# Batch 1's second products as two sweeps over units, weight sums moved forward, and copies of w_in placed behind moves of x

## The chip, the cores and the metric

The kernel runs on one core of one Trainium2 chip. The metric is the device time of one launch in microseconds (us). The engines are TensorE (PE in the profile, with its weight loads as PEld), VectorE (DVE), ScalarE (ACT), GpSimd (POOL) and SyncE (SP), which here only issues DMA transfers. Three timed runs of the kernel before took 632.97 to 633.55 us, median 633.14.

## The reference

An attention between a sequence and a small state, in both directions, and a feed-forward layer on all rows of both results:

```python
B, H, S, Ns, D = (8, 8, 512, 32, 64)
a = softmax(scale * x @ state^T);   xread = a @ state      # rows 0..511 of a batch
a2 = softmax(scale * state @ x^T);  sread = a2 @ x         # rows 512..543
rows = concatenate([xread, sread], axis=2).transpose(0, 2, 1, 3).reshape(B * 544, 512)
h = rows @ w_in                     # 512 -> 2048
g = h * tanh(log(1 + exp(h)))       # mish
out = g @ w_out                     # 2048 -> 512
```

All is fp32 with inputs in memory as 64-bit floats for the weights, which the kernel turns into fp32 by itself.

## The kernel before, in words

Every operand of the two large products is split into a high part, rounded to TensorE's fp32r form, and the low rest; a product is three matmuls (high by high, high by low weights, low by high weights).

xread is never made: state @ w_in is formed per batch (swp in PSUM, from the tiles bd and w_in; parts swh, swl or sw), and the **first product** multiplies it by the softmax weights (tiles ah, al) into the banks ph. There are 8 slots per batch (SLOTS), each of two banks of 128 hidden features for 512 rows: 12 matmuls of 512 columns.

The **second product** goes from mish's output to the banks acc. Batch 0 and batch 1 do it slot by slot for all four blocks of 128 rows (gemm2, line 670): tiles g, gh, gl, half a slot at a time (half_slot, line 1067, and the list `pending`). Later batches do it in two sweeps of 256 rows (p = 0, 1) over **units** (key, p, j): 256 features by 256 rows of slot j. A unit is made by mish (mish_k), prepared (prepare, line 966: high and low parts, tiles gh and gl of tag "g", six buffers) and multiplied (consume, line 1013). A unit in **eight blocks** takes 4 block pairs of 3 matmuls of 512 columns. A unit in **seven products** uses Strassen-like sums: POOL adds blocks of the unit (sums), and 7 products of 3 matmuls of 256 columns replace the 8; in sweeps where all slots are sevens, two matmuls of the seventh product are joined into one of 512 columns (merged). `sevens(key, p)` says how many slots of a sweep are sevens: none in batch 1, 5 in both sweeps of batch 2, 6 and 7 in batch 3's, all 8 later.

Sevens need sums of the weights: seven_weights(j), steps T0 to T7 (line 909). One addition on DVE, four of 256 columns on POOL (j below 4) or DVE, two casts on ACT into the rest of wo and into a tile wx, and the low parts on DVE. The wx of the first slots lies in the buffer of w_in_sb (tag "w_in"), the later ones in those of tags "x" and "sw2". Batches from 2 on read w_in from a copy in DRAM, w_in_again, which four DMAs of 1 MB write (steps w0 and w1 of batch 1, line 1169).

The order of each of PE, DVE, ACT and POOL is the program's order: the class InOrder chains every instruction to the one before it on its engine. Batch 0 follows a list of steps; batches 1 and later follow TABLE (line 1075), one row of steps per slot: G0 and G1 are the halves of the first product, M0 and M1 mish, S and N state @ w_in, X and XD the transposes of x and their moves by eight DMAs (x_turned to x_rows, line 307), SC the scores from x_rows, mm, ee, tr, ex, no, pr the two softmaxes, tu the transposes u and 16 DMAs to e2T, sr the product sread, P and p the preparation of a unit, A and B one half slot or unit each, h and l the high and low part of a slot of batch 1, T the weight sums, w the copies and loads of w_in, lx and li loads of x. Upper case steps belong to the batch that follows. DMA issues on SP have no such chain: a planner orders them from its own estimates, within data dependences and the marks set with `behind(...)`.

Of the kernel before, what the change touches and what calls it, by code (L numbers as in the profile page):

```python
# [9 lines left out]
F32 = mybir.dt.float32  # L10
# [7 lines left out]
P = 128  # L18
# [8 lines left out]
LAG = 2  # L27
WARM = 5
UNITS = 10
SEVEN = 8  # L30
FIRST = 5
G = 4 * P


# [47 lines left out]
def state_attention_mish_kernel(ctx, tc, x, state, w_in, w_out, out):  # L82
# [193 lines left out]
    def attention(b, sn, x_in=None):  # L276
# [689 lines left out]
    def prepare():  # L966
# [46 lines left out]
    def consume():  # L1013
# [8 lines left out]
        if j == max(n7, SLOTS - 2):  # L1022
# [7 lines left out]
        for j, i, hi, lo, a, bank, to, w in steps:  # L1030
# [36 lines left out]
    def half_slot(key, j, at):  # L1067
# [4 lines left out]
        elif ready and (ready[0][:2] != (key, 0) or ready[0][2] < j + (j == SLOTS - 1 and at)):  # L1072
# [1 line left out]

    TABLE = {
        1: """
            G0 M0 G1 M1 z0 z1 mm0 mm1 ee0 ee1 A z0 z1 h l X0 X1 ee0 ee1
            G0 M0 G1 M1 S2 S2 h S2 X2 X3 XD tu w0 B l ST w1
            G0 M0 G1 M1 h A B l
            G0 M0 G1 M1 h A S4 S6 S4 S4 S6 S6 B l T0  # L1080
            G0 M0 G1 M1 h SC sr0 sr1 T0 SC A sr0 sr1 SC MM0 MM1 lx w2 B l T0 TR0 TR1 TR0 TR1 T1
            G0 M0 G1 M1 EE0 EE1 EX0 EX1 T1 h A w3 B l T1 NO EE0 EE1 T2 NO
            G0 M0 G1 M1 h A PR0 PR1 B l
            G0 M0 G1 M1 h PR0 PR1 A N0 PR0 PR1 N0 N0 T2 B l li""",
        2: """
            G0 M0 G1 M1 X0 X1 X2 X3 T2 A T3
            G0 M0 G1 M1 S2 S2 S2 T3 XD B ST T3 A T4
            G0 M0 G1 M1 T4 w4 P p B P p T4 T4
            P G0 M0 p G1 M1 P p A S4 SC S4 S4 SC w5 P p tu B MM0 MM1
            P G0 M0 p G1 M1 P p TR0 TR1 A P TR0 TR1 p B  # L1090
            P G0 M0 p G1 M1 S6 P p S6 S6 EE0 EE1 EX0 EX1 A sr0 sr1 w2 w3 EE0 EE1 P p sr0 sr1 B NO""",
        3: """
            P G0 M0 p G1 M1 P p X0 X1 A P X2 X3 p B
            P G0 M0 p G1 M1 S2 P p S2 S2 XD A ST P p B
            P G0 M0 p G1 M1 P p w4 A P p B
            P G0 M0 p G1 M1 P p A S4 SC S4 S4 SC lx w5 P p B MM0 MM1
            P G0 M0 p G1 M1 P p TR0 TR1 A P TR0 TR1 p T5 B T5
            P G0 M0 p G1 M1 S6 sr0 sr1 P p S6 S6 sr0 sr1 EE0 EE1 EX0 EX1 A w2 w3 EE0 EE1 P p T5 B NO T5
            P G0 M0 p G1 M1 P p NO TU PR0 PR1 A P p B""",
        4: """  # L1100
            P G0 M0 p G1 M1 P p X0 X1 A T6 P X2 X3 p B T6
            P G0 M0 p G1 M1 S2 P p S2 S2 XD A ST T6 P p B
            P G0 M0 p G1 M1 P p T6 w4 A P p B
            P G0 M0 p G1 M1 P p A S4 SC S4 S4 SC lx w5 P p B MM0 MM1
            P G0 M0 p G1 M1 P p TR0 TR1 A P TR0 TR1 p T7 B T7
            P G0 M0 p G1 M1 S6 sr0 sr1 P p S6 S6 sr0 sr1 EE0 EE1 EX0 EX1 A w2 w3 EE0 EE1 P p B T7 NO
            P G0 M0 p G1 M1 P p T7 NO TU PR0 PR1 A P p B""",
        "steady": """
            P G0 M0 p G1 M1 P p X0 X1 A P X2 X3 p B
            P G0 M0 p G1 M1 S2 P p S2 S2 XD A ST P p B  # L1110
# [32 lines left out]
    for key in [*range(1, B - 1), "s", B - 1]:  # L1143
# [22 lines left out]
        def again(n):  # L1166
            if key == 1 and n < 2:
                for g in range(2 * n, 2 * n + 2):
                    nc.sync.dma_start(w_in_again[:, :, g * G:(g + 1) * G], w_in_sb[:, :, g * G:(g + 1) * G])
            else:  # L1170
                of, g = ((key + 1, n - 2), (key, n - 2))[n > 3]
                wis[of, g] = load_w_in_again(g)
# [18 lines left out]
            phs[k] = gemm1(key, j, aTs[key], sw, (k,))[0]  # L1191

        def mish_k(j, k):
            if key == 1:
                if k == 0:
                    gs[j] = new_g(f"1_{j}")
                take_g(gs[j], k, phs[k])
                return
# [5 lines left out]
        def high_1(j):  # L1204
            g = gs.pop(j)
            gs[j] = (g, *high_g(f"1_{j}", g, act.copy))

        def low_1(j):
            g, gh, gl = gs.pop(j)
            low_g(g, gh, gl)  # L1210
            pending.append((1, (2 * j, 2 * j + 1), (gh, gl), NT))
# [56 lines left out]
```

## Time and profile before

| | |
|---|---|
| timed runs, median | 633.14 us (632.97 to 633.55) |
| profiled execution | 633.97 us, span of its instructions 632.1 us |
| PE busy | 623.7 us, 99% |
| PEld busy | 530.3 us, 84% |
| DVE busy | 444.9 us, 70% |
| ACT busy | 357.9 us, 57% |
| POOL busy | 200.5 us, 32% |
| q1, the DMA queue of SP and ACT's issues | 87.58 MB, 44.1% of 16 engines |

Busy time counts a matmul until its modelled end, though the next one has started; so the start times in a timeline tell more of TensorE's pace than busy time does. "idle before <-" names what ended an engine's wait. SPq and ACTq rows are DMA issues: their duration is that of the issue, and the transfer lands later. All instructions stand under line 74, the helper that issues them, so rows are told apart by tiles.

### The profile page before, as it was taken

The page shows a single profiled execution, that of the slowest core. Times are in us where ns is not written, and L with a number is a line of the kernel's source. Part 1 is how long each engine was busy: PE and PEld are TensorE (multiplying, and loading weights), DVE is VectorE, ACT ScalarE, POOL GpSimd, SP SyncE. Part 2 cuts the span into 40 slices and gives each one's busy share as a digit, 9 for nine tenths or more (in the row PEclk, how much of TensorE's full clock was granted, in tenths as well). Part 3 has the DMA queues.
Part 4 walks back from the last instruction along what each step waited for, and adds up shares of the span by engine and source line. Part 5 has one row for each costly group of instructions (what it writes and reads, how often), then busy time and mean ns, then how long its engine had stood idle before and what let it go on. Part 6 is the DMA issues. An engine that isn't in the chain of part 4 may idle for free.

```text
span 632.1 us, 13547 instructions
## 1 busy us (share of the span) xinstructions
PE 623.7 (99%) x5323; PEld 530.3 (84%) x5323; DVE 444.9 (70%) x762; ACT 357.9 (57%) x722; POOL 200.5 (32%) x309
## 2 busy tenths in 40 slices
PE   8999999999999999999999999999999999999997
PEld 6777677787788788888988888888889889898897
DVE  5999786366776873977877873869487777635264
ACT  4999676345465543555447554655456666544442
POOL 0000000123333051323532463336522743443284
PEclk9999999999999999999999999999999999999999
DMA  8999913540465153534554165524555333321000
GB/s 317 412 321 349 324 64 103 139 135 18 106 200 183 34 160 105 171 127 122 142 166 136 33 174 144 181 67 125 143 175 164 106 91 110 101 67 29 7 34 34
DMA packets 71711, 88.77 MB, mean 140 GB/s; under 512 B 13792, under 2 KB 48608, under 8 KB 71648
## 3 DMA queue, kind: packets, MB, share of 16 engines
q1 hardware_dynamic: 71024, 87.58, 44.1%
q8 instruction: 42, 0.69, 0.4%
q10 hardware_dynamic: 624, 0.33, 0.2%
q14 instruction: 21, 0.17, 0.1%
HBM read 62.85 MB, written 13.11 MB: 120 GB/s over the span
## 4 chain that ended last, share of the span: by engine, by line
PE 86%; DMA 5%; DVE 4%; ACT 1%; SPq 1%; issue 1%; POOL 0%; DVEq 0%
PE ph L74 26%; PE acc_top L74 12%; PE acc_one L74 10%; PE acc L74 10%; PE acc_two L74 10%; PE acc_end L74 6%; PE swp L74 5%; PE ph_s L74 3%; DMA w_in_again<-w_in_sb 2%; DMA wir<-in_moe_w_in_dram 2%; DMA wor<-in_moe_w_out_dram 1%; PE srp L74 1%; PE acc_s_one L74 1%; PE acc_s_top L74 1%; PE acc_s_two L74 1%; PE sc L74 1%
## 5 line engine op out<-in xcount | busy, mean ns | idle before, releaser
L74 POOL TENSOR_TENSOR sums<-u 128x256 f32<-128x256 f32 x87 | 70.4, 809 | 230.4 <-DVE gl L74 152.3
L74 ACT ACTIVATE u<-ph 128x256 f32<-128x256 f32 x192 | 63.2, 382 | 85.1 <-PE ph L74 82.9
L74 POOL TENSOR_TENSOR sums<-sums,u 128x128 f32<-128x128 f32 x174 | 100.5, 578 | 13.6
L74 DVE TENSOR_TENSOR gl<-u,gh 128x384 fp32r<-128x384 f32 (+1 forms) x96 | 58.9, 613 | 45.0 <-ACT gh L74 44.1
L74 DVE TENSOR_TENSOR gl<-sums,gh 128x512 fp32r<-128x512 f32 x87 | 66.6, 766 | 29.3 <-ACT gh L74 29.3
L74 PE MATMUL acc<-wo,gh 128*128 128x512 f32 x256 | 80.3, 395 | 0.0
L74 PE MATMUL acc_top<-wo,gh 128*128 128x256 f32 (+1 forms) x384 | 77.8, 294 | 0.0
L74 ACT CAST gh<-u 128x384 fp32r<-128x384 f32 x87 | 44.7, 514 | 55.3 <-PE acc_end L74 38.8
L74 PE MATMUL ph<-ah,swh 128*128 128x512 f32 (+1 forms) x228 | 70.7, 392 | 0.0
L74 PE MATMUL ph<-al,swh 128*128 128x512 f32 (+1 forms) x228 | 70.3, 389 | 0.2 <-DVE al L74 0.2
L74 PE MATMUL ph<-ah,swl 128*128 128x512 f32 (+1 forms) x228 | 70.0, 388 | 0.0
L74 ACT CAST gh<-sums 128x512 fp32r<-128x512 f32 x87 | 54.1, 622 | 26.2 <-POOL sums L74 25.9
L74 PEld LDWEIGHTS acc_top<-wo,gh 128*128 128x128 f32 x384 | 60.5, 191 | 2.7 <-DVE gh L74 0.8
L74 POOL TENSOR_TENSOR w_sums<-w_sums 128x256 f32<-128x256 f32 x16 | 13.0, 811 | 156.3 <-DMA sn<-in_state_dram 123.3
L74 PEld LDWEIGHTS acc<-wo,gh 128*128 128x128 f32 x256 | 47.3, 188 | 13.3 <-issue 3.3
L74 DVE TENSOR_TENSOR swl<-swp,swh 128x512 fp32r<-128x512 f32 (+1 forms) x60 | 36.4, 646 | 29.2 <-ACT swh L74 29.1
L74 PE MATMUL acc_top<-wo,gl 128*128 128x256 f32 (+1 forms) x192 | 56.3, 293 | 0.0
L74 PEld LDWEIGHTS ph<-al,swh 128*128 128x128 f32 x228 | 42.5, 188 | 10.6 <-DVE al L74 1.2
L74 PEld LDWEIGHTS ph<-ah,swl 128*128 128x128 f32 x228 | 42.6, 188 | 9.4 <-DVE swl L74 0.3
L74 PE MATMUL acc<-wo,gl 128*128 128x512 f32 x128 | 49.9, 390 | 0.0
L74 PEld LDWEIGHTS ph<-ah,swh 128*128 128x128 f32 x228 | 39.7, 188 | 8.5 <-issue 0.8
L74 ACT CAST swh<-swp 128x512 fp32r<-128x512 f32 (+1 forms) x60 | 30.5, 562 | 22.7 <-PE swp L74 22.7
(232 smaller groups left out, 1397.5 us busy)
## 6 DMA issues: line engine op xcount, KB each, us to landing
w_in<-w_in_again SPq DMA_DIRECT2D x27, 1024.0 KB, 6.2
x<-in_x_dram SPq DMA_DIRECT2D x32, 256.0 KB, 4.3
wir<-in_moe_w_in_dram SPq DMA_DIRECT2D x16, 512.0 KB, 10.1
wor<-in_moe_w_out_dram SPq DMA_DIRECT2D x16, 512.0 KB, 9.8
x_rows<-x_turned SPq DMA_DIRECT2D x56, 128.0 KB, 2.4
x_in<-in_x_dram SPq DMA_DIRECT2D x24, 256.0 KB, 3.1
out_dram<-sums SPq DMA_DIRECT2D x23, 256.0 KB, 5.3
w_in_again<-w_in_sb SPq DMA_DIRECT2D x4, 1024.0 KB, 9.5
```

Source lines behind the costliest of these rows:

```text
L74: made = method(*args, **kwargs)
```

## The change

- Batch 1 joins the unit scheme: `todo` starts at batch 1, h, l and the tile g go, its mish writes units.
- `sevens`: batch 1 has 0 and 4 (FIRST), batch 2 has 7 and 8, all later sweeps 8.
- All eight-block units get their high part from ACT (before: DVE).
- A sweep without sevens uses two banks only, and its results are copied out of them.
- Weight sums: all subtractions on POOL; T0 to T7 stand between batch 1's slot 3 and batch 3's slot 1 (before: T5 in batch 3, T6 and T7 in batch 4). Tags "x" and "sw2" change places.
- Batch 1's u is made in slot 0 (before: slot 1), and all 16 DMAs to e2T are SP's (before: 4 on ACT). Batch 2's u is made in batch 1's slot 6 (before: batch 2's slot 3).
- The copies w0 and w1 stand behind the last move of x traced before them: w0 behind batch 1's, w1 behind batch 2's.

```diff
-SEVEN = 8
-FIRST = 5
+FIRST = 4
...
-            u = pool.tile([P, 4, 2, NT * NS], F32, tag={0: "u0", 1: "wt", 2: "sw2"}.get(b, "sc"), name=f"u_{b}", bufs=1)
+            u = pool.tile([P, 4, 2, NT * NS], F32, tag={0: "u0", 1: "wt"}.get(b, "sc"), name=f"u_{b}", bufs=1)
...
-                    (nc.scalar if b == 1 and 4 * q + c < 4 else nc.sync).dma_start(
+                    nc.sync.dma_start(
...
-        tag, first, count = ("w_in", 0, 16) if q < 16 else ("x", 16, 4) if q < 20 else ("sw2", 20, 4)
+        tag, first, count = ("w_in", 0, 16) if q < 16 else ("sw2", 16, 4) if q < 20 else ("x", 20, 4)
...
-        by = pool_e if j < 4 else dve
-        if j > 3:
-            yield
-        by.tensor_sub(w[:, 0], w[:, 0], w[:, 1])
...
+        yield
+        pool_e.tensor_sub(w[:, 0], w[:, 0], w[:, 1])
...
-    for key in [*range(2, B - 1), "s", B - 1]:
+    for key in [*range(1, B - 1), "s", B - 1]:
...
     def sevens(key, p):
-        return {2: FIRST, 3: FIRST + 1 + p}.get(key, SEVEN)
+        return {(1, 0): 0, (1, 1): FIRST, (2, 0): SLOTS - 1}.get((key, p), SLOTS)
...
         else:
-            dve.tensor_copy(hi[:, :4], u)
+            act.copy(hi[:, :4], u)
             low_g(u, hi[:, :4], lo[:, :4])
...
-            spans[key, p] = {n: second_bank(f"acc_{key}_{p}_{n}") for n in ("one", "two", "top", "end")}
+            names = ("one", "two", "top", "end")
+            spans[key, p] = {n: second_bank(f"acc_{key}_{p}_{n}") for n in names[0 if sevens(key, p) else 2:]}
...
+        if not sevens(key, t // 2):
+            if "out" not in spans[key, t // 2]:
+                spans[key, t // 2]["out"] = pool.tile([P, 2, DM], F32, tag="g", name=f"o_{key}_{t}", bufs=6)
+            o = spans[key, t // 2]["out"][:, t % 2]
+            (dve.tensor_copy if t % 2 else act.copy)(o, acc)
+            store(key, t, o)
+            return
...
         1: """
-            G0 M0 G1 M1 z0 z1 mm0 mm1 ee0 ee1 A z0 z1 h l X0 X1 ee0 ee1
-            G0 M0 G1 M1 S2 S2 h S2 X2 X3 XD tu w0 B l ST w1
-            G0 M0 G1 M1 h A B l
-            G0 M0 G1 M1 h A S4 S6 S4 S4 S6 S6 B l T0
-            G0 M0 G1 M1 h SC sr0 sr1 T0 SC A sr0 sr1 SC MM0 MM1 lx w2 B l T0 TR0 TR1 TR0 TR1 T1
-            G0 M0 G1 M1 EE0 EE1 EX0 EX1 T1 h A w3 B l T1 NO EE0 EE1 T2 NO
-            G0 M0 G1 M1 h A PR0 PR1 B l
-            G0 M0 G1 M1 h PR0 PR1 A N0 PR0 PR1 N0 N0 T2 B l li""",
+            G0 M0 G1 M1 z0 z1 mm0 mm1 ee0 ee1 A z0 z1 ee0 ee1 tu X0 X1
+            P G0 M0 p G1 M1 w0 S2 S2 S2 X2 X3 XD B ST w1
+            P G0 M0 p G1 M1
+            P G0 M0 p G1 M1 S4 S6 A S4 S4 S6 S6 T0 T0
+            P G0 M0 p G1 M1 SC sr0 sr1 SC A sr0 sr1 SC MM0 MM1 w2 lx TR0 TR1 TR0 TR1
+            P G0 M0 p G1 M1 T0 EE0 EE1 EX0 EX1 A T0 P p w3 B NO EE0 EE1 NO T1 T1
+            P G0 M0 p G1 M1 A P p TU PR0 PR1 T1 T1 B
+            P G0 M0 p G1 M1 N0 PR0 PR1 T2 T2 P p N0 N0 PR0 PR1 A T2 li P p T2 B""",
         2: """
-            G0 M0 G1 M1 X0 X1 X2 X3 T2 A T3
-            G0 M0 G1 M1 S2 S2 S2 T3 XD B ST T3 A T4
-            G0 M0 G1 M1 T4 w4 P p B P p T4 T4
...
+            P G0 M0 p G1 M1 T3 P p T3 X0 X1 A P X2 X3 p B T3
+            P G0 M0 p G1 M1 S2 T3 P p S2 S2 XD A ST P p B
+            P G0 M0 p G1 M1 P p w4 A T4 P p T4 B
+            P G0 M0 p G1 M1 T4 P p A S4 SC S4 S4 SC w5 P p T4 B T5 MM0 MM1
...
+            P G0 M0 p G1 M1 P p X0 X1 A P X2 X3 p T7 B
+            P T7 G0 M0 p G1 M1 S2 P p S2 S2 XD A T7 ST P p T7 B
...
                 for g in range(2 * n, 2 * n + 2):
-                    nc.sync.dma_start(w_in_again[:, :, g * G:(g + 1) * G], w_in_sb[:, :, g * G:(g + 1) * G])
+                    with behind("move"):
+                        nc.sync.dma_start(w_in_again[:, :, g * G:(g + 1) * G], w_in_sb[:, :, g * G:(g + 1) * G])
```

## Rows read from the trace of the kernel before

**Rows 1.** Two stretches of the table of busy times (stretch and length in us, then busy us and instructions of PE, PEld, DVE, ACT and POOL, the granted clock as a share, the DMA engines' share and GB/s), and the longest wait of PE between 15 and 500 us (us in total, times, longest).
```profile
100.00:180.00 80.00, 80.00 (x573) 63.03 (x558) 51.08 (x82) 38.58 (x70) 19.42 (x24) 1.00 0.39 111
180.00:340.00 160.00, 160.00 (x1491) 137.70 (x1490) 121.04 (x217) 83.17 (x192) 49.58 (x80) 1.00 0.46 135
...
PE sc L74 <- DMA x_rows<-x_turned: 1.2, 2, 0.7
```

**Rows 2.** The same table for three shorter stretches.
```profile
36.00:62.00 26.00, 26.00 (x140) 20.12 (x139) 24.40 (x33) 25.78 (x29) 0.00 (x0) 1.00 1.00 352
62.00:66.00 4.00, 2.82 (x38) 1.29 (x36) 2.98 (x3) 3.40 (x6) 0.00 (x0) 1.00 0.63 139
...
104.00:120.00 16.00, 16.00 (x127) 12.62 (x126) 5.43 (x9) 6.41 (x11) 0.00 (x0) 1.00 0.47 132
```

**Rows 3.** Timeline of PE (start us, length us, engine, line, operation, tiles, count): the first row of two half slots of batch 1 and the row behind them, and the same for a unit in seven products of a later batch.
```profile
106.38 0.62 PE L74 MATMUL acc<-wo,gh 128*128 128x512 f32 x2
...
111.82 0.62 PE L74 MATMUL ph<-ah,sw 128*128 128x512 f32 x2
...
303.40 0.40 PE L74 MATMUL acc_one<-wo,gh 128*128 128x256 f32 x2
...
305.92 0.63 PE L74 MATMUL ph<-ah,swh 128*128 128x512 f32 x2
```

**Rows 4.** Timeline of SP's DMA issues: two copies of w_in, and batch 1's moves of x.
```profile
36.28 0.64 SPq L1169 DMA_DIRECT2D w_in_again<-w_in_sb  x1
...
48.93 0.56 SPq L1169 DMA_DIRECT2D w_in_again<-w_in_sb  x1
...
54.09 9.05 SPq L307 DMA_DIRECT2D x_rows<-x_turned  x8
```

**Rows 5.** The chain of waits between 55 and 100 us (start, length, what).
```profile
48.93 12.31 DMA w_in_again<-w_in_sb
...
66.88 7.42 DMA wor<-in_moe_w_out_dram
...
80.39 1.42 PE swp L74 x32
```

**Rows 6.** SP's issues of batch 2's moves and of 12 of batch 1's transfers to e2T, and the time from issue to landing of the moves between 50 and 190 us.
```profile
104.15 5.51 SPq L307 DMA_DIRECT2D x_rows<-x_turned  x8
109.77 7.53 SPq L404 DMA_DIRECT2D e2T<-u  x12
...
DMA to landing us min/median/max: 2.3/2.5/8.0
```

**Rows 7.** Timeline of PE around batch 1's scores.
```profile
62.83 0.39 PE L74 MATMUL acc<-wo,gl 128*128 128x512 f32 x1
63.91 0.59 PE L74 MATMUL sc<-x_rows,bd 64*32 64x256 f32 x2 [0.69 <-DMA x_rows<-x_turned]
64.99 1.09 PE L74 MATMUL sc<-x_rows,bd 64*32 64x256 f32 x30 [0.49 <-DMA x_rows<-x_turned]
```

**Rows 8.** Timeline of DVE in batch 1's first two slots: batch 0's srds, the first of four small steps, and batch 1's u.
```profile
96.43 0.47 DVE L74 TENSOR_SCALAR srds<-srp,rs 128x64 f32<-128x64 f32 x2
...
101.11 0.11 DVE L74 TENSOR_SCALAR sm<-sm 128x1 f32<-128x1 f32 x1
...
104.04 1.26 DVE L74 STREAM_TRANSPOSE u<-e 128x512 f32<-128x512 f32 x2
```

**Rows 9.** Timeline of PE: slot 2's first product, the two swp of slot 3, and batch 2's first product.
```profile
103.66 0.62 PE L74 MATMUL ph<-ah,sw 128*128 128x512 f32 x2
...
117.36 1.96 PE L74 MATMUL swp<-w_in_sb,bd 64*32 64x256 f32 x64
...
158.30 0.77 PE L74 MATMUL ph<-ah,swh 128*128 128x512 f32 x2
```

**Rows 10.** Timeline of ACT: a table load, the last two of the four exps behind it, ah, the longer cast of a weight sum, and the mish of a half slot of batch 2.
```profile
136.12 1.28 ACT L74 ACT_TABLE_LOAD   x1
...
138.84 1.14 ACT L74 ACTIVATE e<-e 128x512 f32<-128x512 f32 x2
...
156.41 1.14 ACT L74 CAST ah<-at 128x512 fp32r<-128x512 f32 x2
...
158.72 0.84 ACT L74 CAST wx_w_in<-w_sums 128x768 fp32r<-128x768 f32 x1
...
160.15 0.66 ACT L74 ACTIVATE u<-ph 128x256 f32<-128x256 f32 x2 [0.59 <-PE ph L74]
```

**Rows 11.** Timeline of POOL: two of its groups for the weight sums.
```profile
124.61 3.17 POOL L74 TENSOR_TENSOR w_sums<-w_sums 128x256 f32<-128x256 f32 x4 [123.31 <-DMA sn<-in_state_dram]
...
151.60 4.37 POOL L74 TENSOR_TENSOR w_sums<-w_sums 128x256 f32<-128x256 f32 x4 [8.33 <-DVE w_sums L74]
```

**Rows 12.** Timeline of DVE: the reduce that begins the first softmax's sums, the two multiplications by the reciprocals, the addition of a weight sum, and al.
```profile
147.46 0.68 DVE L74 TENSOR_REDUCE s<-e 128x16 f32<-128x512 f32 x1
...
149.13 0.69 DVE L74 TENSOR_TENSOR e<-e,r 128x512 f32<-128x512 f32 x1
...
150.25 1.20 DVE L74 TENSOR_TENSOR w_sums<-wo 128x1024 f32<-128x1024 f32 x1
...
151.65 1.23 DVE L74 TENSOR_TENSOR e<-e,r 128x512 f32<-128x512 f32 x1
...
157.06 1.29 DVE L74 TENSOR_TENSOR al<-at,ah 128x512 fp32r<-128x512 f32 x2 [1.69 <-ACT ah L74]
```

More of the change, by code (lines that the diff above doesn't have):

```diff
@@ L913, in seven_weights @@
             w.rearrange("p (k e) c -> p k (e c)", k=2), as_f32(wo[j][:, :, 0]), as_f32(wo[j][:, :, 1]))
-        by = pool_e if j < 4 else dve
-        if j > 3:
-            yield
-        by.tensor_sub(w[:, 0], w[:, 0], w[:, 1])
-        by.tensor_sub(w[:, 1], w[:, 3], w[:, 1])
-        by.tensor_add(w[:, 3], w[:, 3], w[:, 0])
-        by.tensor_sub(w[:, 2], w[:, 2], w[:, 3])
+        yield
+        pool_e.tensor_sub(w[:, 0], w[:, 0], w[:, 1])
+        pool_e.tensor_sub(w[:, 1], w[:, 3], w[:, 1])
+        pool_e.tensor_add(w[:, 3], w[:, 3], w[:, 0])
+        pool_e.tensor_sub(w[:, 2], w[:, 2], w[:, 3])
         yield
@@ L1000, in sums_of @@
     def sums_of(key, p, banks):
-        tag, bufs = ("g", 6) if (key, p) in ((B - 3, 1), (B - 2, 0)) else ("wt", 1)
+        tag, bufs = ("g", 6) if (key, p) in ((1, 1), (B - 3, 1), (B - 2, 0)) else ("wt", 1)
         e = banks["sums"] = pool.tile([P, 4, 256], F32, tag=tag, name=f"sums_{key}_{p}", bufs=bufs)
@@ L1018, in consume @@
         if j == 0:
-            spans[key, p] = {n: second_bank(f"acc_{key}_{p}_{n}") for n in ("one", "two", "top", "end")}
+            names = ("one", "two", "top", "end")
+            spans[key, p] = {n: second_bank(f"acc_{key}_{p}_{n}") for n in names[0 if sevens(key, p) else 2:]}
         banks = spans[key, p]
         n7 = sevens(key, p)
-        if j == max(n7, SLOTS - 2):
+        if n7 and j == max(n7, SLOTS - 2):
             sums_of(key, p, banks)
@@ L1044, in consume @@
             if j == SLOTS - 1 and i == (5 if n7 > j else 1):
-                late.append((key, 2 * p, banks["top"], banks["sums"][:, ::2], ALU.add))
+                late.append((key, 2 * p, banks["top"], n7 and banks["sums"][:, ::2], ALU.add))
             if j == SLOTS - 1 and i == (6 if n7 > j else 3):
-                late.append((key, 2 * p + 1, banks["end"], banks["sums"][:, 1::2], ALU.subtract))
+                late.append((key, 2 * p + 1, banks["end"], n7 and banks["sums"][:, 1::2], ALU.subtract))
             if (key, p) != (B - 2, 0):
@@ L1085, in state_attention_mish_kernel @@
-        2: """
-            G0 M0 G1 M1 X0 X1 X2 X3 T2 A T3
-            G0 M0 G1 M1 S2 S2 S2 T3 XD B ST T3 A T4
-            G0 M0 G1 M1 T4 w4 P p B P p T4 T4
-            P G0 M0 p G1 M1 P p A S4 SC S4 S4 SC w5 P p tu B MM0 MM1
-            P G0 M0 p G1 M1 P p TR0 TR1 A P TR0 TR1 p B
-            P G0 M0 p G1 M1 S6 P p S6 S6 EE0 EE1 EX0 EX1 A sr0 sr1 w2 w3 EE0 EE1 P p sr0 sr1 B NO""",
-        3: """
[L1093 to L1107, printed above, removed]
+            G0 M0 G1 M1 z0 z1 mm0 mm1 ee0 ee1 A z0 z1 ee0 ee1 tu X0 X1
@@ new lines, in state_attention_mish_kernel @@
+            P G0 M0 p G1 M1 w0 S2 S2 S2 X2 X3 XD B ST w1
[5 more added lines that the diff above has]
+            P G0 M0 p G1 M1 N0 PR0 PR1 T2 T2 P p N0 N0 PR0 PR1 A T2 li P p T2 B""",
+        2: """
+            P G0 M0 p G1 M1 T3 P p T3 X0 X1 A P X2 X3 p B T3
+            P G0 M0 p G1 M1 S2 T3 P p S2 S2 XD A ST P p B
+            P G0 M0 p G1 M1 P p w4 A T4 P p T4 B
+            P G0 M0 p G1 M1 T4 P p A S4 SC S4 S4 SC w5 P p T4 B T5 MM0 MM1
+            P T5 G0 M0 p G1 M1 P p TR0 TR1 A T5 P TR0 TR1 p T5 B
+            P G0 M0 p G1 M1 S6 sr0 sr1 P p S6 S6 sr0 sr1 EE0 EE1 EX0 EX1 A T6 w2 w3 EE0 EE1 P T6 p B NO
+            P G0 M0 p G1 M1 P p T6 NO T6 TU PR0 PR1 A P p B
+            P G0 M0 p G1 M1 N0 PR0 PR1 P p N0 N0 PR0 PR1 A li P p B""",
@@ L1108, in state_attention_mish_kernel @@
+        3: """
+            P G0 M0 p G1 M1 P p X0 X1 A P X2 X3 p T7 B
+            P T7 G0 M0 p G1 M1 S2 P p S2 S2 XD A T7 ST P p T7 B
+            P G0 M0 p G1 M1 P p w4 A P p B""",
         "steady": """
@@ L1193, in mish_k @@
         def mish_k(j, k):
[L1194 to L1198, printed above, removed]
             for p in range(2):
@@ L1202, in mish_k @@
                     u[:, 1 - k].rearrange("f h t -> f (h t)"), phs[k][:, p * 2 * P:(p + 1) * 2 * P], AF.Mish)
[L1204 to L1211, printed above, removed]
         def visit_sw(i):
@@ L1220, in state_attention_mish_kernel @@
             run = {
-                "G": lambda k: first_k(j, k), "M": lambda k: mish_k(j, k), "h": lambda _: high_1(j), "l": lambda _: low_1(j),
+                "G": lambda k: first_k(j, k), "M": lambda k: mish_k(j, k),
                 "P": lambda _: begin(), "p": lambda _: end(),
```

## The prediction

> **What bounds the kernel now.** I read the page's busy shares first, then the table of stretches, then TensorE's own waits, then the chain of waits where TensorE did wait, and only then the timelines of single engines. The reader is to see that TensorE is the bound nearly everywhere: 80.00 of 80 us between 100 and 180, 160.00 of 160 in the stretch behind it, always at a granted clock of 1.00, the upper of its two levels (2.4 GHz) [rows 1]. Between 15 and 500 us its only wait worth naming is 1.2 us for the turned rows of x [rows 1]. Since a busy matmul row overlaps the next one, I price TensorE by the distance between starts and not by busy time.
>
> Two things can therefore change the time: matmuls that disappear, and waits of TensorE that appear or go. The stretch from 36 to 66 us is the one with a visible wait, and there the DMA engines are full: share 1.00 at 352 GB/s from 36 to 62 us [rows 2].
>
> **Part 1, seven products instead of eight.** A unit in eight blocks costs 12 matmuls of 512 columns. Two of them run from 106.38 to 111.82, so 2.72 us each. A unit in seven products costs 21 matmuls of 256 columns, 303.40 to 305.92, 2.52 us [rows 3]; the form that joins two of its matmuls has the same columns, and I take the same price. So each unit that changes form gives 0.20 us. Units in eight blocks before: 16 of batch 1 (eight slots, each worth two units), 3 and 3 of batch 2, 2 and 1 of batch 3, together 25. After: 8 in batch 1's first sweep, 4 in its second, 1 in batch 2's first, together 13. Twelve units at 0.20 us are **2.4 us** off TensorE. All of them lie where TensorE has no gap, so all 2.4 us count unless something new is late.
>
> **Part 2, the copies of w_in.** Three of the four 1 MB copies are issued between 36.28 and 48.93 us, ahead of the eight moves of x that begin at 54.09 [rows 4]. At the 352 GB/s of that stretch each holds the DMA engines for 1.05/0.352 = 3.0 us. The third lands 12.31 us after its issue, at 61.24, and the chain of waits goes from it straight into SP's moves [rows 5]. The moves take 9.05 us to issue, where batch 2's eight take 5.51 in a quiet stretch [rows 4, 6]. Without the copies ahead of them the moves still can't start before 54.09, when DVE has just made the last x_turned, but then end near 59.6 and land 2.5 later [rows 6], about 62.1. TensorE wants them at 63.16: the matmul that starts at 62.83 holds it for 0.23, and the change of form takes 0.1. Before, the scores start at 63.91, break off after two instructions (0.07) and resume at 64.99: 0.75 + 1.01 = **1.8 us** of stall that can go [rows 7].
>
> What is late next? The same chain goes on from SP through the last load of w_out (wor, 7.42 us to land), ACT and DVE, to TensorE's swp at 80.39 [rows 5]. TensorE can keep its 1.8 us at 80 only if that load lands as much earlier. It stands behind the moves (same buffer), which end 3.5 us earlier on SP (63.14 against 59.6). If SP puts the two released copies right behind the moves, they take some 5.8 us of DMA time, of which the stretch from 62 to 66 us (share 0.63, 139 GB/s [rows 2]) can take a part; my estimate is that wor lands 1 to 4 us earlier. I take the full 1.8; bounds 0 and 2.2, the upper one with 0.4 lost around 80.39, where swp takes 1.42 us instead of about 1.1.
>
> The other two copies now follow batch 2's moves near 115 us, where the DMA share is 0.47 [rows 2]. Nothing on TensorE stands behind them but T0's write, which is a rival below.
>
> **Part 3, batch 1's new order.** Four units (10.9 us of TensorE) go out of batch 1 into batch 2, so ACT, DVE and SP have that much less cover in batch 1. Two deadlines decide, both on the clock of before.
>
> *Batch 2's moves.* The transposes u now stand in slot 0, before x's: DVE ends srds at 96.9, then some 0.5 of small steps and 1.26 for u, so u is ready at 98.7 instead of 105.3; x's transposes end near 104.1 as before [rows 8]. SP then issues 16 of e2T at 7.53/12 = 0.63 us (four of them stood on ACT's queue) to 108.9, and the moves behind them, 5.5 us, the last landing near 116.4 [rows 6]. On TensorE slot 2 starts at 103.66, a first product takes 2.72 (to 106.38); then another one, swp at 1.96, a unit at 2.8 and a third first product: scores at 116.7 [rows 3, 9]. Slack 0.3 us. If SP mixes in two stores, 0.5 us each, the stall is 0.7; if the moves overtake e2T, none. I take 0.2.
>
> *The end of batch 1.* The longest chain I find, in program order: slot 5's last mish can start at 124.6; T0's casts 1.1, table load and exps 3.9, a cast 0.6 [rows 10]; DVE: a low part 0.7, the sums' reduces and reciprocals 3.7, T1's addition 1.2 [rows 12]; POOL 3.17 [rows 11]; ACT: T1's casts 1.1, four mish 1.3, ah 1.1, a cast 0.5, swh 1.0 [rows 10]; DVE: the rest of swl 1.4 and al 1.2 [rows 12]: 146.5. Batch 2's first product starts at 147.4 (158.30 less 10.9 [rows 9]), and needs al 0.45 later. Slack 1.3 us, so no stall; bounds 0 and 3 us, if POOL's groups and DVE's long instructions stretch. ACT also takes over a 0.6 us cast per eight-block unit from DVE and loses four DMA issues; both lie under TensorE here.
>
> *POOL.* The subtractions of T4 to T7 go from DVE to POOL at 3.17 us a slot [rows 11], and four more units want its sums; batch 2 is over 65 us long, and POOL was busy 49.58 of 160 us [rows 1]. Cost 0, DVE being relieved by about as much; with the cover gone, 1 us a slot. In the rows POOL's group at 151.60 took 4.37 us, not 3.17, while DVE's multiplication of two SBUF tiles took 1.23 instead of 0.69 [rows 11, 12]. The Trainium skill (SBUF — State Buffer, Who interferes with whom) has a rule for it: a DVE instruction with two SBUF inputs and a GpSimd instruction that reads SBUF exclude each other; the trace agrees. By that rule the work given to POOL costs DVE too, and the time would be rival 2's.
>
> **The sum.** 2.4 + 1.8 - 0.2 = 4.0 us. The profiled execution took 633.97 us, its span 632.1; it becomes 629.97. The median of the timed runs is 633.14, 0.83 below that execution, so I forecast **629.1 us**.
>
> **The rivals.**
> 1. *The copies give nothing*: wor lands no earlier, and TensorE gives the 1.8 us back at 80.39, or SP's order keeps other loads ahead of the moves. For it: the chain through wor [rows 5]. Against it: three copies less in the queue. Then 2.4 stays: 630.7.
> 2. *Batch 1 gets too short for ACT, DVE and POOL*: POOL's groups at 4.37 instead of 3.17, twice on the chain to al and to the first sevens, and three DVE instructions that stretch by 0.5, 3.9 us in all, less 1.3 of slack: 2.5 us of stall, 631.6. For it: the stretched rows [rows 11, 12]. Against it: POOL is busy 19.42 of 80 us in that stretch, ACT 38.58 [rows 1].
> 3. *Slower: T0 waits for the late copies.* T0's casts write the buffer of w_in_sb, which the two copies behind batch 2's moves still read. ACT reaches T0 at 125.2; every us that they land later goes down the chain above, past its 1.3 us of slack. Issued at 115 they land by 122 at 3.0 us each. Behind a full queue, at the 12.31 us of the third copy [rows 5], and after SP's loads of sn, w_in and x (issued from 118 on before), it is 134: 134 - 125.2 - 1.3 = 7.5 us, 633.14 - 4.0 + 7.5 = 636.6. It decides from a landing at about 132 on. Against it: the share of 0.47 [rows 2].
>
> **How the numbers follow.** Chances: forecast 0.46, rival 1 0.22, rival 2 0.20, rival 3 0.12. A measurement here tells changes over 0.2%, 1.3 us, so faster is under 631.87. The forecast and nearly all of rival 1 are faster, rival 2 (631.6, give or take 1.5) about half: 0.46 + 0.21 + 0.10 = 0.77. The same: 0.01 + 0.09 + 0.03 = 0.13. Slower: 0.01 + 0.09 = 0.10. The range runs from 1 us under the forecast (the 0.4 at 80 us, 0.6 for a stall that I don't see) to 632.6, which holds most of rival 2.
>
> **What would show it.** Right: no wait for x_rows near 63 us; swp near 80 at 1.1 us; batch 2's scores without a stall; batch 2's first product about 12.7 us earlier than at 158.30 (10.9 moved, 1.8 gained); 2.4 us less TensorE time in second products. Wrong: TensorE waiting for al, gl or x_rows between 100 and 165 us; ACT waiting for a w_in_again copy; wor landing at 74 again.

## The result and the profile after

The changed kernel takes 637.39 us (six executions, 635.20 to 638.72) where the kernel before takes 632.99 beside it: ratio 1.0063, 95% interval 1.0044 to 1.0082. It is slower by some 4 us, and the forecast was 4 us faster. A second comparison on another chip (the run a_again below) gave 1.0076, 1.0060 to 1.0092. The profiled execution took 638.72 us, span 636.9.

All helper rows now stand under line 73, SP's moves under 306, the copies of w_in under 1165. First the page's shares, which answer to the table of before:

```profile
PE 624.0 (98%) x5407; PEld 533.7 (84%) x5407; DVE 449.1 (71%) x764; ACT 369.1 (58%) x767; POOL 240.1 (38%) x361
```

Then TensorE's waits between 100 and 230 us (what waited for what: total us, times, longest), and the table of stretches that answers to [rows 1], with the stretch behind the longest wait apart:

```profile
PE acc_one L73 <- DVE wx_w_in L73: 2.1, 1, 2.1
PE acc_top L73 <- ACT gh L73: 1.1, 1, 1.1
PE srp L73 <- ACT u L73: 0.8, 1, 0.8
PE acc_end L73 <- DVE o L73: 0.5, 1, 0.5
PE sc L73 <- issue: 0.3, 1, 0.3
PE acc_one L73 <- DVE gl L73: 0.2, 1, 0.2
```

```profile
100.00:180.00 80.00, 76.79 (x559) 61.83 (x558) 51.41 (x83) 39.72 (x89) 29.84 (x38) 0.98 0.50 148
180.00:340.00 160.00, 158.06 (x1464) 137.09 (x1462) 121.74 (x206) 88.80 (x201) 77.53 (x114) 1.00 0.41 124
...
166.00:171.00 5.00, 5.00 (x23) 4.41 (x22) 3.22 (x5) 1.04 (x3) 0.32 (x1) 0.66 0.46 97
```

Before, TensorE was busy for all of the first two stretches; now 3.2 and 1.9 us are missing, behind DVE and ACT, and in five microseconds the mean granted clock is 0.66. PE's timeline at the places of [rows 7], [rows 5] and [rows 9]:

```profile
63.47 1.09 PE L73 MATMUL sc<-x_rows,bd 64*32 64x256 f32 x32
...
79.02 1.11 PE L73 MATMUL swp<-w_in_sb,bd 64*32 64x256 f32 x32
...
115.09 0.62 PE L73 MATMUL sc<-x_rows,bd 64*32 64x256 f32 x2
116.02 1.09 PE L73 MATMUL sc<-x_rows,bd 64*32 64x256 f32 x30 [0.31 <-issue]
...
146.65 0.62 PE L73 MATMUL ph<-ah,swh 128*128 128x512 f32 x2
```

Batch 1's scores are one row of 32 without a break, swp near 80 takes 1.11 us instead of 1.42, and batch 2's first product starts 11.65 us earlier (12.7 forecast). SP's issues that answer to [rows 4, 6] show the moves of both batches, with the copies behind them:

```profile
54.33 6.04 SPq L306 DMA_DIRECT2D x_rows<-x_turned  x8
...
61.57 0.61 SPq L1165 DMA_DIRECT2D w_in_again<-w_in_sb  x1
...
96.98 11.06 SPq L403 DMA_DIRECT2D e2T<-u  x16
108.14 5.21 SPq L306 DMA_DIRECT2D x_rows<-x_turned  x8
...
114.72 1.29 SPq L1165 DMA_DIRECT2D w_in_again<-w_in_sb  x2
```

Batch 1's moves are issued by 60.4 instead of 63.1. Batch 2's stand behind sixteen e2T transfers and end at 113.35, where TensorE reaches the scores at 115.09; their landing costs it 0.9 us. Up to here the forecast holds but for that. The loss lies in batch 2. Batch 3's first product, before and now:

```profile
219.11 0.62 PE L74 MATMUL ph<-ah,swh 128*128 128x512 f32 x2
...
224.84 0.62 PE L73 MATMUL ph<-ah,swh 128*128 128x512 f32 x2
```

From batch 2's first product to this took 60.8 us before (from 158.30) and takes 78.2 now (from 146.65), where 60.8 plus the 10.9 moved in, less 1.2 saved there (six units that change form), would be 70.5. The largest piece is seen in TensorE's timeline around unit (1,1,3):

```profile
162.88 0.38 PE L73 MATMUL acc_one<-wx_w_in,gh 128*128 128x256 f32 x1
165.32 0.38 PE L73 MATMUL acc_one<-wx_w_in,gh 128*128 128x256 f32 x1 [2.06 <-DVE wx_w_in L73]
...
168.03 1.05 PE L73 MATMUL ph<-ah,swh 128*128 128x512 f32 x2
168.89 1.05 PE L73 MATMUL ph<-al,swh 128*128 128x512 f32 x2
...
170.84 0.62 PE L73 MATMUL ph<-al,swh 128*128 128x512 f32 x2
```

One matmul that reads the high part of slot 3's weight sum runs, and the next, which reads the low part, comes 2.44 us later instead of 0.12. Behind it, pairs of 512 columns take 1.05 us instead of 0.62: from about 166.7 to 170.1 us the granted clock was at its lower level (1.2 GHz), which costs half of that, 1.7 us. What the low part waited for stands on POOL, ACT and DVE (with T2's group and al, the rows that answer to [rows 11, 12]):

```profile
142.61 3.85 POOL L73 TENSOR_TENSOR w_sums<-w_sums 128x256 f32<-128x256 f32 x4 [3.26 <-DVE w_sums L73]
...
155.40 3.77 POOL L73 TENSOR_TENSOR w_sums<-w_sums 128x256 f32<-128x256 f32 x4 [1.16 <-DVE w_sums L73]
159.12 0.73 POOL L73 TENSOR_TENSOR sums<-u 128x256 f32<-128x256 f32 x1
159.93 1.20 POOL L73 TENSOR_TENSOR sums<-sums,u 128x128 f32<-128x128 f32 x2
```

```profile
161.16 0.62 ACT L73 CAST gh<-sums 128x512 fp32r<-128x512 f32 x1 [5.86 <-POOL sums L73]
161.69 0.40 ACT L73 CAST wo<-w_sums 128x256 fp32r<-128x256 f32 x1
162.00 0.83 ACT L73 CAST wx_w_in<-w_sums 128x768 fp32r<-128x768 f32 x1
162.73 0.61 ACT L73 CAST gh<-u 128x512 fp32r<-128x512 f32 x1
```

```profile
145.02 1.99 DVE L73 TENSOR_TENSOR al<-at,ah 128x512 fp32r<-128x512 f32 x2
...
153.85 1.47 DVE L73 TENSOR_TENSOR w_sums<-wo 128x1024 f32<-128x1024 f32 x1
...
155.71 1.22 DVE L73 TENSOR_TENSOR gl<-sums,gh 128x512 fp32r<-128x512 f32 x1
...
161.81 0.69 DVE L73 TENSOR_TENSOR gl<-sums,gh 128x512 fp32r<-128x512 f32 x1 [1.55 <-ACT gh L73]
163.38 0.69 DVE L73 TENSOR_TENSOR gl<-u,gh 128x512 fp32r<-128x512 f32 x1 [0.87 <-ACT gh L73]
163.99 0.42 DVE L73 TENSOR_TENSOR wo<-w_sums,wo 128x256 fp32r<-128x256 f32 x1
164.32 0.95 DVE L73 TENSOR_TENSOR wx_w_in<-w_sums,wx_w_in 128x768 fp32r<-128x768 f32 x1
```

POOL's group for T3, the one at 155.40, ended at 159.17. But ACT's order puts the cast of unit (1,1,3)'s sums first, and those end on POOL at 161.13; T3's casts follow, then the cast and the low part of unit (1,1,4), and only then T3's low parts, ready at 165.27. So T3 lost 2.5 us on ACT, behind a cast that itself waited for POOL, and 1.2 on DVE, behind a low part that TensorE reads only from 172.21 us on.

Between the distances of starts, the two profiled executions give (us): part 1 -2.8, the start of batch 1 -1.7, batch 2's scores +0.9, units (1,1,0) and (1,1,1) +1.3, T3 +2.3, the clock +1.7, srp near 199 +0.9, unit (2,0,7) near 220 +1.3: +3.9 of the 4.9 by which TensorE's last matmul starts later. One microsecond stays unassigned.

### The profile page after: what moved, and what is told of

Read it like the earlier page. It is cut to its first block, busy times and chain, and to the rows that moved or that the text cites. A ratio compares the mean times of both kernels' runs of the same rounds, so it can differ in the third digit from the quotient of the medians.

```text
span 636.9 us, 13849 instructions
## 1 busy us (share of the span) xinstructions
PE 624.0 (98%) x5407; PEld 533.7 (84%) x5407; DVE 449.1 (71%) x764; ACT 369.1 (58%) x767; POOL 240.1 (38%) x361
## 4 chain that ended last, share of the span: by engine, by line
PE 74%; DVE 9%; POOL 4%; ACT 3%; issue 2%; DVEq 0%; ACTq 0%; POOLq 0%
PE ph L73 22%; PE acc_top L73 11%; PE acc_one L73 10%; PE acc_two L73 10%; PE acc_end L73 6%; PE swp L73 4%; PE acc L73 3%; PE ph_s L73 3%; POOL w_sums L73 2%; DVE gl L73 2%; POOL sums L73 1%; PE srp L73 1%; DVE w_sums L73 1%; PE acc_s_one L73 1%; PE sc L73 1%
## 5 line engine op out<-in xcount | busy, mean ns | idle before, releaser
L73 DVE TENSOR_TENSOR gl<-u,gh 128x384 fp32r<-128x384 f32 (+1 forms) x112 | 71.2, 635 | 75.8 <-ACT gh L73 73.5
L73 POOL TENSOR_TENSOR sums<-sums,u 128x128 f32<-128x128 f32 x198 | 116.2, 587 | 15.5
L73 DVE TENSOR_TENSOR gl<-sums,gh 128x512 fp32r<-128x512 f32 x99 | 79.1, 799 | 36.6 <-ACT gh L73 36.6
L73 ACT CAST gh<-u 128x384 fp32r<-128x384 f32 (+1 forms) x112 | 58.9, 525 | 65.8 <-PE acc_end L73 53.1
L73 PE MATMUL acc_top<-wo,gh 128*128 128x256 f32 (+1 forms) x448 | 92.1, 297 | 1.1 <-ACT gh L73 1.1
L73 POOL TENSOR_TENSOR w_sums<-w_sums 128x256 f32<-128x256 f32 x32 | 27.5, 860 | 165.0 <-DMA x_rows<-x_turned 111.7
L73 PEld LDWEIGHTS acc_top<-wo,gl 128*128 128x128 f32 x224 | 42.9, 191 | 1.5 <-DVE gl L73 0.4
L73 PE MATMUL acc_one<-wo,gh 128*128 128x256 f32 x198 | 41.9, 293 | 0.0
L73 PEld LDWEIGHTS acc_one<-wo,gh 128*128 128x128 f32 x198 | 32.1, 189 | 10.0 <-ACT u L73 3.7
L73 PE MATMUL acc<-wo,gh 128*128 128x512 f32 x128 | 40.4, 396 | 0.0
```

What stands on the lines that cost most here:

```text
L73: made = method(*args, **kwargs)
```

## The experiments

Twelve runs; each ratio is to the kernel before, run beside it on the same chip (medians 632.27 to 632.55 us there).

**The copies of w_in.** b_copies puts only part 2 into the kernel before; a_nobehind takes only part 2 out of the changed kernel (the edit shown; b_copies has its reverse).

```diff
-                    with behind("move"):
-                        nc.sync.dma_start(w_in_again[:, :, g * G:(g + 1) * G], w_in_sb[:, :, g * G:(g + 1) * G])
+                    nc.sync.dma_start(w_in_again[:, :, g * G:(g + 1) * G], w_in_sb[:, :, g * G:(g + 1) * G])
```

> The kernel before, with nothing of the change but the copies of w_in placed behind the moves of x (part 2 alone). Theory (the step of the prediction holds): the stall of 1.8 us at batch 1's scores near 63 us goes and nothing gives it back, so 633.0 - 1.8 = about 631.2 us, with batch 1's scores free of waits and wor landing near 72.4 us instead of 74.3. Rival (rival 1 of the prediction): the 1.8 us come back at swp near 80 us or at a later wait, so 633.0 give or take 0.4.

> The changed kernel without part 2: three of the four copies of w_in stand ahead of batch 1's moves again. Theory (part 2's gain of 1.7 us reaches the end of the changed kernel too): 637.4 + 1.7 = about 639.1 us, with the wait of about 1.8 us at the scores near 63 us back. Rival: the waits of batch 2 are set by ACT, DVE and POOL and not by TensorE's start, so what is lost at 63 us is made up there: 637.4 give or take 0.6.

b_copies: 634.25 us, ratio 1.0025 (1.0015 to 1.0035): slower, against both theories. The stall at 63 us is gone and batch 1's first product starts at 88.43, as forecast, but ACT shows why nothing is left of it:

```profile
124.85 0.40 ACT L74 CAST wo<-w_sums 128x256 fp32r<-128x256 f32 x1
130.66 0.83 ACT L74 CAST wx_w_in<-w_sums 128x768 fp32r<-128x768 f32 x1 [5.41 <-DMA w_in_again<-w_in_sb]
```

T0's cast comes before the late copies land, all of ACT queues behind it, and batch 2's first product then waits 1.34 us for swh. That is rival 3's mechanism, in the kernel that the forecast didn't try it on. But the run isn't part 2 alone: in the old table both copy steps stand behind batch 2's moves, so all four copies are issued late, two at 115.56 us and two at 119.56. The changed kernel has only two there, from 114.72 on. They landed by 123.73, 1.0 us ahead of T0's cast into their buffer (124.69), and no row shows a wait for them.

a_nobehind: 637.09 us, ratio 1.0069 (1.0054 to 1.0084), not to be told from the changed kernel. Its stall at the scores was only 0.7 us, and its batch 1 starts no later (88.41 us, where the changed kernel has 88.50). So b_again takes a second trace of the kernel before:

> The kernel before itself, for a second profiled execution of it. Theory (the execution that the prediction was worked out from had a longer stall at batch 1's scores than most): a stall there of about 0.6 us, as in the changed kernel without part 2, and not 1.8. Rival (the stall is 1.8 us in this kernel whenever it runs, and something else in the changed kernel shortens it): 1.8 us again.

```profile
62.64 0.39 PE L74 MATMUL acc<-wo,gl 128*128 128x512 f32 x1
63.34 0.59 PE L74 MATMUL sc<-x_rows,bd 64*32 64x256 f32 x2 [0.31 <-DMA x_rows<-x_turned]
64.25 1.09 PE L74 MATMUL sc<-x_rows,bd 64*32 64x256 f32 x30 [0.33 <-DMA x_rows<-x_turned]
```

Reckoned as the forecast did, 0.4 + 0.8 = 1.2 us, between the two theories, in an execution of 632.95 us. The stall isn't a constant: 1.8 and 1.2 in two executions of the kernel before, and 0.7 in each of the two versions of the changed kernel without part 2 (a_nobehind, and a_all_nb below), which differ from it in more.

**The deadlines of the weight sums.** a_first3 and a_first0 set FIRST, the number of sevens in batch 1's second sweep, to 3 and 0. The weight sums are still written over half of wo at their old places, so unit (1,1,3), or units (1,1,0) to (1,1,3), read sums there and not w_out: these two kernels leave out the order that a right result needs, and serve for times alone. Their instructions are those of eight blocks.

```diff
-FIRST = 4
+FIRST = 3
```

> The changed kernel with three sevens instead of four in batch 1's second sweep (unit (1,1,3) in eight blocks, which needs no weight sum of slot 3). Theory (TensorE's wait of 2.06 us for T3's low parts, and the fall of the granted clock right behind it, are one cause and cost about 2.3 + 1.7 us): 637.4 + 0.2 - 2.3 - 1.7 = about 633.6 us, and a mean granted clock of 1.000 in every run. Rival (DVE and POOL are behind in that stretch as a whole, so the next unit waits instead): 636.5 to 637.6 us, with a wait of over 1.5 us elsewhere between 150 and 180 us. Second rival (the clock's fall has nothing to do with the wait): about 635.3 us with a clock of 0.997 in some runs.

> The changed kernel with no sevens in batch 1's second sweep: eight blocks for all eight units, so the first weight sum is needed by batch 2's first sweep only. Work on TensorE 4 x 0.20 = 0.8 us more. Theory (the three weight sums that are due early are what costs): the wait of 2.3 us, the clock's 1.7 us and the 1.3 us around unit (1,1,0) go: 637.4 + 0.8 - 5.3 = about 632.9 us, clock 1.000. Rival (POOL and DVE are too slow for batch 2 whatever the deadline): 636 us or more, with new waits of TensorE for wx_w_in, gh or gl in batch 2.

a_first3: 634.76 us (633.51 to 635.90), ratio 1.0028 (1.0015 to 1.0040), clock 0.999 or 1.000 in all ten executions. The wait is gone and no other takes its place; the first theory holds for the wait and the clock. The profiled execution, 633.84, is the size expected, but the median is 1.2 us above the theory, and why the longer executions took up to 2 us more no trace shows. a_first0: 633.23 us, ratio 1.0010 (1.0001 to 1.0019), 0.3 us above the theory, or 0.7 with this chip's kernel before (632.55) in place of 632.99; the waits at 149 to 153 and at 163 are gone. A wait of 1.4 us near 214, for gh, stays, and a new one of 0.9 near 211 is for a weight sum of T6, a wait of the kind that the rival names.

**Only the order.** a_t3 moves two steps of the table:

```diff
-            P G0 M0 p G1 M1 T3 P p T3 X0 X1 A P X2 X3 p B T3
-            P G0 M0 p G1 M1 S2 T3 P p S2 S2 XD A ST P p B
+            P G0 M0 p G1 M1 T3 P p T3 X0 X1 A P X2 X3 T3 T3 p B
+            P G0 M0 p G1 M1 S2 P p S2 S2 XD A ST P p B
```

> The changed kernel with T3's casts and low parts ahead of the second half of the preparation of unit (1,1,3) instead of behind it and behind that half slot; nothing else moves. Theory (it is the order on ACT and DVE that makes T3 late: its casts stood behind a cast that waits for POOL's sums of (1,1,3)): casts at 159.2 instead of 161.7, low parts done by 161.7 instead of 165.3, TensorE's wait of 2.3 us and the clock's fall behind it go: 637.4 - 2.3 - 1.7 = about 633.4 us, ratio to before about 1.001. Rival (POOL is too slow, whatever the order): TensorE then waits for unit (1,1,3)'s gl as long, 636 to 637.5 us, ratio 1.005 or more.

633.54 us, ratio 1.0014 (1.0000 to 1.0029); clock 0.999 or 1.000 in all ten. DVE shows the new order:

```profile
158.40 0.88 DVE L73 TENSOR_TENSOR wo<-w_sums,wo 128x256 fp32r<-128x256 f32 x1
159.20 1.21 DVE L73 TENSOR_TENSOR wx_w_in<-w_sums,wx_w_in 128x768 fp32r<-128x768 f32 x1
160.34 0.81 DVE L73 TENSOR_TENSOR gl<-u,gh 128x384 fp32r<-128x384 f32 x1
161.43 0.69 DVE L73 TENSOR_TENSOR gl<-sums,gh 128x512 fp32r<-128x512 f32 x1 [0.27 <-ACT gh L73]
```

T3's low parts are done at 160.4, and TensorE reads them at 161.97 without a wait. Two steps, four instructions in all, moved by some places are worth 3 to 4 us; POOL's group still takes its 3.8 us, so it wasn't POOL's speed.

a_t456 moves T4's last two steps, T5 and T6 forward by about a row of batch 2:

```diff
-            P G0 M0 p G1 M1 P p w4 A T4 P p T4 B
-            P G0 M0 p G1 M1 T4 P p A S4 SC S4 S4 SC w5 P p T4 B T5 MM0 MM1
-            P T5 G0 M0 p G1 M1 P p TR0 TR1 A T5 P TR0 TR1 p T5 B
+            P G0 M0 p G1 M1 P p w4 A T4 P p T4 B T4
+            P T4 G0 M0 p T5 G1 M1 P p T5 A S4 SC S4 S4 SC w5 T5 P p B T5 MM0 MM1
+            P G0 M0 p G1 M1 P p TR0 TR1 A P TR0 TR1 p B T6
...
```

> The changed kernel with T4's casts and low parts, and all of T5 and T6, moved forward by about one row of batch 2's table; T3 stays. Theory (T5's group on POOL delays the sums behind it and with them ACT, and T6's low parts delay DVE's transposes and with them unit (2,0,7)'s gh): the waits of 0.9 us near 199 and 1.3 us near 220 go and T3's 2.3 us stays: 637.4 - 2.2 = about 635.2 us, ratio about 1.003. Rival (the engines are full there and the waits only change place): 637.4 give or take 0.7, ratio 1.006.

635.83 us, ratio 1.0044 (1.0029 to 1.0058): the waits near 199 and 220 are gone, T3's 2.3 us and the clock's fall (0.996 or 0.997 in six of nine executions) stay. It gives 1.2 us against the one comparison of the changed kernel and 2.0 against the other; 2.2 were expected.

**Is it POOL's or DVE's work?** a_dvesub gives the subtractions of T4 to T7 back to DVE, in place:

```diff
-        pool_e.tensor_sub(w[:, 0], w[:, 0], w[:, 1])
+        by = pool_e if j < 4 else dve
+        by.tensor_sub(w[:, 0], w[:, 0], w[:, 1])
...
```

> The changed kernel with the four subtractions of T4 to T7 on DVE, as before; all places stay. Theory (POOL's groups of T5 and T6 delay the sums behind them; on DVE they take about half): the waits of 0.9 us near 199 and 1.3 us near 220 shrink, ratio about 1.003 where the changed kernel has 1.006. Rival (DVE is the engine that is late there, and gets 1.7 us more per slot): the same 1.006 or up to 1.009, with longer waits near 199 and 220.

> The changed kernel itself, to stand beside the others of this call on one chip. By the first comparison: ratio 1.006, with a granted clock of 0.996 to 0.997 in the longer executions and 0.999 or 1.000 in the shorter ones. Rival: another chip's executions don't show this split.

a_dvesub: 639.51 us, ratio 1.0109 (1.0094 to 1.0125); a_again beside it 637.12, with clocks of 1.000, 0.997, 0.997 and 1.000, so the split shows on this chip too. The wait near 199 is gone, as the theory says, but the time is past even the rival's 1.009: the wait near 220 goes from 1.1 to 1.3, T7's group makes swl late in batch 3, and T3's wait, ahead of all the moved work, from 2.1 to 2.6. TensorE's longest waits from 100 to 260 us, then T3's last low part on DVE:

```profile
PE acc_one L73 <- DVE wx_w_in L73: 2.6, 1, 2.6
PE acc_top L73 <- ACT gh L73: 1.3, 1, 1.3
PE ph L73 <- DVE swl L73: 0.8, 1, 0.8
...
```

```profile
164.34 1.48 DVE L73 TENSOR_TENSOR wx_w_in<-w_sums,wx_w_in 128x768 fp32r<-128x768 f32 x1
```

In the changed kernel that low part takes 0.95 us. Here POOL, which has no T4 group to wait for, adds the blocks of a later unit beside it (164.27 to 165.01), and the clock fell in all four executions. So in this order of steps POOL is the better place for the subtractions. That DVE is the engine short of time, as the rival says, isn't shown apart from T3's wait and the clock.

**Putting it together.** a_all has both moves of the table, T2's low parts behind batch 1's last half slot, and four e2T transfers on ACT again. a_all_nb is the same without part 2.

> The changed kernel with both of these, and with T2's low parts behind the last half slot of batch 1 (so that DVE copies o from the bank 1.9 us earlier) and four of the sixteen transfers to e2T on ACT's queue again. Theory (the change's two gains are real and only the order of the weight sums loses them): 637.4 - 4.0 (T3 and clock) - 2.2 (T4 to T6) - 0.7 (o) - 0.6 (e2T) = about 629.9 us, ratio to before about 0.995. Rival (ACT, DVE and POOL can't carry the weight sums in this time in any order): over 632 us, with new waits in batch 2.

> The kernel of the run before without part 2 (three of the four copies of w_in ahead of batch 1's moves). Theory (part 2 is worth 1.7 us once nothing behind it waits): 1.7 us above that kernel, about 631.6 us, ratio to before about 0.9975, with a wait at the scores near 63 us. Rival (as the changed kernel without part 2 showed: a wait of about 0.5 us there, and batch 1's first product not later): within 0.6 us of that kernel.

a_all: 631.69 us, ratio 0.9984 (0.9972 to 0.9996), faster than before, yet 1.8 us short of the theory. Batch 2's scores run without a break, but T2's move only changed who waits: o is copied in time, and the low parts of units (1,1,0) and (1,1,1) are late, 0.37 + 1.04 + 0.40 = 1.8 us between 148 and 153. a_all_nb: 632.60, ratio 1.0000 (0.9984 to 1.0015). Part 2 is worth 0.9 us here, half the forecast; without it the ten executions spread over 2.3 us, with it over 1.0.

a_best moves T1 and T2 in batch 1 too:

```diff
-            P G0 M0 p G1 M1 T0 EE0 EE1 EX0 EX1 A T0 P p w3 B NO EE0 EE1 NO T1 T1
-            P G0 M0 p G1 M1 A P p TU PR0 PR1 T1 T1 B
-            P G0 M0 p G1 M1 N0 PR0 PR1 T2 T2 P p N0 N0 PR0 PR1 A T2 li P p T2 B""",
+            P G0 M0 p G1 M1 T0 EE0 EE1 EX0 EX1 A T0 T1 P p w3 B T1 NO EE0 EE1 NO
+            P G0 M0 p G1 M1 A P p T1 T1 TU PR0 PR1 T2 B
+            P G0 M0 p T2 G1 M1 N0 PR0 PR1 P p N0 N0 PR0 PR1 A T2 T2 li P p B""",
```

> As a_all, but T1 and T2 stand earlier in batch 1 as well: T1's addition right behind T0's low parts (DVE idled 3.4 us there), its casts and low parts ahead of the transposes u, T2's addition behind them, T2's low parts ahead of those of unit (1,1,0). Theory (the 1.8 us of waits that a_all kept between 148 and 153 us, 0.37 + 1.04 + 0.40, come from T2's late place alone): ratio to before 0.9984 - 1.8/632.5 = about 0.9956, or 629.8 us where before takes 632.5, and no wait of TensorE over 0.3 us from 100 to 500 us but the changes of form. Rival (T1 and T2 now collide with al or with e's multiplications, and batch 2's first product is late): ratio 0.998 or more, with a wait for al, gh or gl between 125 and 155 us.

629.94 us (629.41 to 630.19), ratio 0.9958 (0.9946 to 0.9971). The theory's 0.9956 is met. No wait of TensorE is listed between 100 and 230 us, and the stretches of [rows 1] are full again, with POOL as busy as in the changed kernel:

```profile
100.00:180.00 80.00, 80.00 (x643) 64.80 (x642) 58.95 (x92) 45.96 (x103) 32.75 (x43) 1.00 0.51 150
180.00:340.00 160.00, 160.00 (x1494) 140.05 (x1493) 120.40 (x214) 91.66 (x203) 75.17 (x113) 1.00 0.44 135
```

Its batch 2 takes 70.5 us (145.21 to 215.73), as worked out above. This version beats both kernels, by 2.3 us (2.7 by the ratio) where the kernel before is concerned. That is still less than the 4.0 that the change was priced at, since its two gains are smaller than booked, as the next section says.

## Why the prediction was wrong

**Part 1 was right.** The trace counts 1372 matmuls of 512 columns and 1971 of 256 before, 1252 and 2175 after; starts lie 0.227 and 0.120 us apart: 120 x 0.227 - 204 x 0.120 = 2.8 us. Some 0.3 of this is the joined form in 24 more units, which the forecast priced like the other. By starts, a_best takes 196.74 us from batch 1's first product to batch 4's (87.95 to 284.69) and b_again 198.91 (89.11 to 288.02): 2.2 us less, near the 2.4 of the forecast.

**Part 2 had the right mechanism and a wrong size.** The term "I take the full 1.8" came from one execution, itself 0.83 us above the median, as the text said. Four traces of the stall give 0.7 to 1.8, and the pair a_all and a_all_nb 0.9 us. wor did land earlier (72.44 instead of 74.30) and swp came down to 1.11, so rival 1's mechanism fell. Rival 3 didn't happen here: the copies landed at 119.65 and 123.73. b_copies, with four late copies, shows that it was no idle rival.

**Part 3 failed, at the sentence "Two deadlines decide".** Of the two that it names, batch 2's moves cost 0.9 us where the sum has 0.2. The other held: al, forecast for 146.5, was ready at 147.01, 0.1 us before TensorE's matmul with it (147.11). There was no stall, but next to nothing was left of the slack of 1.3, with POOL's group at 3.85 us and the two al at 1.99.

But each seven needs its slot's weight sum, and an eight must be multiplied before that sum is written over its half of wo. These are further deadlines, T0 to T3 for units (1,1,0) to (1,1,3) and T6 for the end of batch 2, each fixed by a place in the table. The sum laid out none of them. T3's was missed, which cost 2.3 us and the clock's 1.7. T2, T5 and T6 were in time, but stood on DVE or POOL ahead of other work that was then late, 3.5 us in all (1.3 at units (1,1,0) and (1,1,1), 0.9 and 1.3 near 199 and 220). Moving these steps takes the waits away: T3's in a_t3, the last two in a_t456, all of them in a_best. Of the signs of failure that the forecast listed, ACT's wait for a copy and wor at 74 didn't come; the longest wait, for wx_w_in, wasn't on the list. T3's time can be worked out from rows of before: an addition of 1.20, a POOL group of 3.17 to 4.37, casts, low parts, and whatever stands ahead of each on its engine.

**"Cost 0, DVE being relieved by about as much" failed with it.** The step compared busy shares (POOL 49.58 of 160 us). No engine was full: POOL was busy 77.53 of 160 us in the changed kernel's trace and nearly as long, 75.17, in a_best's. What cost 3 to 4 us was the place of T3's four casts and low parts (a_t3). The fallback of "1 us a slot" had neither the cause nor the place. The move of the subtractions to POOL is not what lost the time: with those of T4 to T7 back on DVE the kernel is slower still (a_dvesub, 1.0109 against 1.0076).

**Rival 2 named the engines and not the mechanism.** It put the stall at al and the first sevens and priced it at 2.5 us. It left the waits at the other sums out, and the clock, which the forecast held at 1.00 throughout.

The Trainium skill's rule in the forecast (SBUF — State Buffer, Who interferes with whom), that a DVE instruction with two SBUF inputs and a GpSimd instruction that reads SBUF exclude each other, is borne out again by stretched rows: T3's group took 3.77 us, and DVE's low part beside it 1.22 (155.71) where one alone took 0.69 (161.81). In a_dvesub such a stretch, 1.48 us for 0.95, lengthens TensorE's wait by 0.5. Were it the cause of the loss, a_best would be about as slow as the changed kernel, since it runs as many instructions on both engines; it is 7 us faster.

## What to carry to other kernels

Where a change makes work depend on something prepared, list every consumer with its deadline and follow each chain through the program's order on every engine, counting what stands ahead of it; busy shares don't see that. In an order written by hand, a step's place is part of its price: put the cast and the low part that are needed first ahead of those that wait for a later result. And size a stall from more than one execution before it is booked as a gain.

## What the hardware showed that was not expected

The wait of 2 us could cost nearly as much again. In the five kernels whose trace has it, 19 of 27 executions show a mean granted clock of 0.996 or 0.997; in the other eight run here, all 65 show 0.999 or 1.000. Among the ten executions of the changed kernel the six at 0.997 average 637.86 us and the four at 1.000 average 636.04: 1.8 us, near the 1.7 worked out from the rows. The same wait doesn't always lower the clock: the traces of a_again, a_nobehind and a_t456 have it too, 2.1 us long, and stay at the upper level behind it, as in this stretch of a_again:

```profile
165.00:170.00 5.00, 5.00 (x30) 4.39 (x29) 3.21 (x5) 1.89 (x5) 0.77 (x2) 1.00 0.43 93
```

In a_dvesub, whose trace has a wait of 2.6 us, it fell in all four executions. What decides it, no run here shows. The Trainium skill (TensorE: Matmul & The Clock Gate, HAM oscillation — how this bites in real kernels) describes a wait that throws TensorE back to its lower clock, so that the next work starts slow. a_dvesub's trace agrees, where the first matmul behind the wait takes 0.58 us instead of 0.38; in the changed kernel's rows the fall comes 1.4 us after the wait, and in the three traces above not at all.
